# One pool for all eight PSUM banks, and MLP gelus joined to the next mixer gelu, in a planned two-layer attention and mixer kernel

## The chip, the cores and the metric

The kernel runs on one core of a Trainium2 chip. The metric is the device time of one execution in microseconds (us). The kernel before was run three times: 1471.07, 1471.91 and 1472.3 us. Its engines are called PE (matrix products; PEld is its weight load), ACT (ScalarE, table functions), DVE (VectorE), POOL (GpSimd) and SP, which only issues DMAs here.

## What is computed

Two layers, each an attention block and a mixer block, on an input of 2048 rows by 512. The attention has 32 query heads of width 16 and one shared key and value head. The mixer shifts quarters of its features by 1, -1, 2 and -2 rows and ends in an MLP of width 1792. Everything is bf16 at the borders.

```python
def _A_ref(x, wq, wk, wv, wo):                 # S=2048, D=512, H=32, Dh=16
    q = transpose((x @ wq).reshape(B, S, H, Dh), 0, 2, 1, 3)
    k = x @ wk
    v = x @ wv
    scores = einsum("bhqd,bkd->bhqk", q, k) * (Dh ** -0.5)
    p = softmax(scores)
    o = einsum("bhqk,bkd->bhqd", p, v)
    return transpose(o, 0, 2, 1, 3).reshape(B, S, H * Dh) @ wo

def _B_ref(x, w1, w2, w3, w4):
    h = gelu(layernorm(x) @ w1)
    # g0..g3: quarters of h, shifted by 1, -1, 2, -2 rows
    hs = concatenate([g0, g1, g2, g3]) @ w2
    x1 = x + hs
    h2 = gelu(layernorm(x1) @ w3) @ w4
    return x1 + h2

for layer in range(2):
    x = x + _A_ref(layernorm(x), ...)
    x = x + _B_ref(layernorm(x), ...)
```

## The kernel before

**Tiling.** The 2048 rows are 16 tiles of 128. A layer works in chunks of query rows: four of 512 in layer 1, three of 512 and two of 256 in layer 2 (`CHUNKS`, L536). A chunk is eight blocks of four heads (`b`), a block runs over 16 key tiles (`kb`), and each key tile is two halves (`p`) of two heads. A half is therefore 128 keys by 512 queries for two heads: two score matmuls into two PSUM banks of 512 fp32 columns. There are 2048 halves in all.

**Two ways to an exponential.** A half goes one of two ways. As a *unit* (`declare_unit`, L1111) its two score matmuls (L1083, in the profile `PB<-QT,KT`) fill two neighbouring banks and one ACT instruction over 1024 columns writes exp to `EA` (L1127). As a *pair* (`declare_pair`, L1133) each of its two banks is evicted by DVE into a 16-bit integer (`J<-PB`, L1145), which read as bf16 is a rough exponential; two further terms come from integer additions on `J` (`shift_op`, L1182, on POOL, or on DVE while POOL has enough queued), and the three terms are weighted by scaled copies of the values (`VD`). Then the value products (L1232) of both kinds add into one PSUM bank, `ACC`, until the block's last key tile is in.

**The end of a block** (`block_end`, L1240). DVE copies `ACC` to `ACCF` (or adds it to a spilled partial sum: the first chunk of layer 2 starts on early key tiles before layer 1 has ended, L1024 to L1039). Small matmuls (L1285) and a reciprocal turn the sums into factors, DMAs bring the rows into `OT`, and `scale_pair` applies the factors.

**The end of a chunk** (`chunk_end`, L1447). When all eight blocks are in, the rest of the layer for these rows is declared: the output projection, the mixer's first product and gelu (`mixer_in`: W1 products at L676, evicted to `GP` at L1531, one gelu over 4 x 512 columns at L1535), the second product (`mix`), and the MLP (`mlp`: W3 products evicted to `G2` at L1610, a gelu per tile over 1792 columns at L1615, W4 products in `mlp_out`), then, in layer 1, the next layer's keys and values (`next_kv`). A mixer shift needs rows of the next chunk, so the MLP of a chunk covers the tiles that are ripe: three, four, four, then the rest. In the last chunk of layer 2 (`tail`) the gelus read PSUM directly. Exp and gelu need different tables, so a change between them costs a load (`ACT_TABLE_LOAD`).

**Who sets the order.** Nothing of this is a fixed loop. `Plan` is a list scheduler in Python: it keeps modelled clocks of the engines, picks for each engine that is free the ready operation of least priority value, and writes one static instruction stream per engine with semaphore waits. `_pick` (L204) chooses: scores of units have priority 0, scores of pairs 0.5, value products 2, a chunk's projections 10 or less. `limits` and `due` (L291, L306) keep PE from starting work that would make a unit's scores late. `filler` (L1089) adds dummy matmuls (`PB<-ONES,NIL`) when PE's modelled activity falls short. `assign` (L1414) decides when a half becomes a pair, by thresholds that change every 12.5 planned us: the string `TEMPER` (L590) names one of 16 sets of thresholds (`MOODS`) for each stretch.

**Banks.** PSUM has eight banks. Units alternate between banks 0, 1 and 2, 3 (`ACT_SLOTS`); bank 4 is `ACC`, the only accumulator; banks 5, 6 and 7 are a pool for everything else: pair scores, projections, transposes. An operation that takes a bank from the pool (`take`) is placed only when one has been given back (`give`) for a margin of 0.15 us. When all attention work is placed, the units' banks and `ACC` are lent to the pool (`lend`, L317).

Of the kernel before, what the change touches and what calls it, by code (L numbers as in the profile page):

```python
# [27 lines left out]
class Op:  # L28
    __slots__ = ("eng", "emit", "preds", "npend", "succ", "dur", "prio", "seq", "ready", "start",
                 "end", "take", "give", "dma", "out", "pos", "sem", "vc", "side", "placed", "pe", "feeds", "port", "parts", "after", "entry", "weight")  # L30


class Plan:
# [31 lines left out]
    CLOSE = 2.5  # L65
# [4 lines left out]
    BODY = 0.2  # L70

    def __init__(self, nc, pool_banks):
# [29 lines left out]
        self.loose = False  # L102

    def op(self, eng, emit, reads=(), writes=(), dur=0.1, prio=None, take=None, give=None,
# [8 lines left out]
        o.feeds = None  # L113
# [90 lines left out]
    def _pick(self, eng, t, dense=False):  # L204
# [3 lines left out]
        limit = self.limits(t) if eng == "PE" and not dense else ()  # L208
        joins = eng == "PE" and t < self.pe_end - 1e-9
        low = self.deferred(h, t, joins) if eng == "PE" and not dense else {}  # L210
        pressing = joins and any(o.prio == 0 and o.ready <= t + 1e-9 for o in h) and self.pe_kind != "Q"
# [3 lines left out]
        due = list(limit) + self.due(h, t) if stick else ()  # L215
# [4 lines left out]
        for o in h:  # L220
# [13 lines left out]
            key = (low.get(o, o.prio), o.seq)  # L234
            if self.CLOSE and eng == "PE" and o.prio > 2 and o not in low and o.take is None:
                key = (self.CLOSE, o.seq)
# [7 lines left out]
            if o.take is not None:  # L244
                if not all(p.placed and (p.end <= t + 1e-9 or p.eng == "PE") for p in o.take.gates):
                    continue
                margin = self.MARGIN if o.side else self.LAT["PE"]
                k = sorted(i for i in range(len(self.pool)) if self.pool[i][0] + margin <= t + 1e-9)
                k = sorted(sorted(k, key=lambda i: self.pool[i][0])[:o.take.n])
                if len(k) < o.take.n or o.prio > 2 and len(self.pool) <= self.SPARE and self.attach is not None and not self.loose:  # L250
                    continue
# [6 lines left out]
        if o.take is not None:  # L258
            got = [self.pool[i][1] for i in bank]
            for i in reversed(bank):  # L260
                self.pool.pop(i)
            o.take.bank = got[0] if o.take.n == 1 else tuple(sorted(got))
# [28 lines left out]
    def limits(self, t):  # L291

        x = max(t, self.free_at["ACT"])
        res = []
        late = {}
        for u in self.units[-4:]:
            if not u.placed:
                late[u] = x
                x += u.dur
        for o in self.heap["PE"]:  # L300
            if o.prio == 0 and o.ready > t + 1e-9 and o.feeds in late:
                d = late[o.feeds] - o.pe[1] / (2400.0 if self.warm else 1200.0) - 0.17 - self.LAT["ACT"]
                res.append(max(o.ready, d) + self.SLACK)
        return res

    def due(self, h, t):  # L306

        x = max(t, self.free_at["ACT"])
        late = {}
        for u in self.units[-4:]:  # L310
            if not u.placed:
                late[u] = x
                x += u.dur
        return [late[o.feeds] - o.pe[1] / (2400.0 if self.warm else 1200.0) - 0.17 - self.LAT["ACT"]
                for o in h if o.prio == 0 and o.ready <= t + 1e-9 and o.feeds in late]

    def lend(self, banks, o):  # L317

        for b in banks:
            self.pool.append((o.end, b))  # L320
            self.pool_last[b] = o
        heapq.heappush(self.events, o.end + self.MARGIN)
# [187 lines left out]
def t_ps(n):  # L510
    return 0.066 + n * 1.043e-3
# [22 lines left out]
class Kernel:  # L534
# [9 lines left out]
    ACT_SLOTS = (0, 2)  # L544
    ACC = 4
    POOL_BANKS = (5, 6, 7)
# [8 lines left out]
    CALM_END = (2, 1)  # L555
    LATE_OT = 6
# [8 lines left out]
    FREE = 2  # L565
# [24 lines left out]
    TEMPER = "090e357fe7f4ff7e0f7e2eeeff72790e3f75e5ff7145fe87e4c1e43707f90000548fe5eeef9f07ece7eeeff1f0ef9fefee4f897fe741eccccccccc"  # L590
# [1091 lines left out]
```

## Time and profile before

| | us | how to read it |
|---|---|---|
| profiled execution | 1472.13 | one execution, recorded instruction by instruction |
| its span | 1470.2 | first to last instruction; 1.9 lie around it |
| exps, L1127, x1406 | 1292.9 busy | ACT time covered by them; they overlap, one lasts 1.17 on average |
| MLP gelus, L1615, x29 | 47.0 busy | 128 x 1792 each |
| mixer gelus, L1535, x8 | 14.4 busy | seven of 128 x 2048, one of 128 x 1024 |
| table loads, x30 | 38.6 busy | 14 before exps, 8 before mixer gelus, 7 before MLP gelus, one at the start; 1.283 each |
| pair evictions, L1145, x1284 | 821.8 busy | DVE, 0.68 each in the row, overlapping |
| shifts on POOL, L1182, x534 | 976.6 busy | 489 of two rows at 1.90, 45 of one row at 1.06 |
| shifts on DVE, L1182, x136 | 98.6 busy | 125 of two rows at 0.72, 11 of one row at 0.80 |
| fillers, L676 `PB<-ONES,NIL`, x532 | 49.2 busy | dummy matmuls, four at a time |
| first exp starts | 13.99 | |
| last exp ends | 1409.33 | |

Busy time counts an instant once, however many instructions of a group overlap in it, so busy time over count is the step from one to the next where a group runs without gaps, and the mean length of one is longer. The granted clock of PE is 1.00 in every stretch of the run. POOL and DVE do not share work except the shifts.

### The profile page before, as it was taken

Reading aid. Unit: us, or ns where it says so; the run is one execution under the profiler, and the core shown is the slowest. Engines: PE = TensorE matmul, PEld = TensorE weight load, DVE = VectorE, ACT = ScalarE, POOL = GpSimd, SP = SyncE. Lnnn points to the kernel's source line nnn. Section 1 sums busy time; section 2 is a strip of 40 time slices with the busy share of each in tenths; the row PEclk is TensorE's granted clock in tenths of the full one; section 3 lists DMA queues with packets and bytes.
Section 4 is the critical chain, followed back from the end, with each engine's and each line's share of the span. In section 5 each row is a group of like instructions: output and inputs, shape, how many; then the busy total and the mean of one; then the engine's idle time right before and its main releaser. Section 6 shows DMA issues by size and latency. Waiting matters only on the chain.

```text
span 1470.2 us, 65395 instructions
## 1 busy us (share of the span) xinstructions
PE 1446.2 (98%) x29813; PEld 646.8 (44%) x29813; DVE 1295.5 (88%) x2323; ACT 1406.4 (96%) x1496; POOL 1140.3 (78%) x830
## 2 busy tenths in 40 slices
PE   9999999999999999999999999999999999999999
PEld 4344334444443444444444444444433344555565
DVE  8899999989999889998987899999989998889873
ACT  7999999999999999999979999999999999999962
POOL 2888887878898778899854789789769968788951
PEclk9999999999999999999999999999999999999999
DMA  6100100001000000100000000010000000000000
GB/s 217 31 6 6 20 5 7 6 5 20 6 6 5 6 4 6 21 6 2 3 3 3 3 10 10 6 21 5 9 18 8 4 6 8 20 15 7 8 15 24
DMA packets 32662, 21.76 MB, mean 15 GB/s; under 512 B 13056, under 2 KB 31872, under 8 KB 32384
## 3 DMA queue, kind: packets, MB, share of 16 engines
q1 hardware_dynamic: 32384, 17.57, 5.2%
q8 instruction: 233, 3.82, 1.1%
q14 instruction: 45, 0.37, 0.1%
HBM read 7.90 MB, written 2.10 MB: 7 GB/s over the span
## 4 chain that ended last, share of the span: by engine, by line
ACT 73%; PE 22%; DVE 3%; POOL 2%; issue 0%; POOLq 0%
ACT EA L1127 68%; PE PB L676 8%; PE PB L1083 6%; PE PB L1232 6%; ACT G L1615 2%; POOL J L1182 1%; ACT L1127 1%; DVE J L1145 1%; ACT GP L1535 1%; PE PB L876 1%; ACT L1535 1%; ACT L1615 1%; DVE G L1610 0%; PE PB L933 0%; DVE J L1182 0%
## 5 line engine op out<-in xcount | busy, mean ns | idle before, releaser
L1127 ACT ACTIVATE EA<-PB 128x1024 bf16<-128x1024 f32 x1406 | 1292.9, 1172 | 12.3 <-PE PB L1083 6.1
L1182 POOL TENSOR_SCALAR J<-J 128x2048 uint16<-128x2048 uint16 (+1 forms) x534 | 976.6, 1829 | 213.9 <-DVE J L1182 90.1
L1145 DVE TENSOR_SCALAR J<-PB 128x512 uint16<-128x512 f32 x1284 | 821.8, 681 | 81.6 <-PE PB L1083 77.5
L1083 PE MATMUL PB<-QT,KT 32*128 32x512 bf16 (+1 forms) x4608 | 603.0, 360 | 11.7 <-ACT EA L1127 5.0
L1232 PE MATMUL PB<-J,VD 128*32 128x256 bf16 (+1 forms) x8628 | 418.5, 265 | 3.0 <-POOL J L1182 1.1
L1232 PE MATMUL PB<-EA,VP 128*32 128x256 bf16 (+1 forms) x6340 | 343.8, 263 | 1.0 <-DVE QT L1244 0.3
L1083 PEld LDWEIGHTS PB<-QT,KT 32*128 32x128 bf16 x4608 | 162.6, 91 | 383.6 <-ACT EA L1127 313.1
L1232 PEld LDWEIGHTS PB<-J,VD 128*32 128x32 bf16 x8628 | 179.0, 95 | 180.5 <-issue 131.1
L1232 PEld LDWEIGHTS PB<-EA,VP 128*32 128x32 bf16 x6340 | 147.6, 95 | 111.1 <-issue 91.0
L676 PE MATMUL PB<-ZT,W 128*32 128x512 bf16 (+2 forms) x2816 | 168.7, 342 | 0.6 <-DVE ZT L885 0.3
L1182 DVE TENSOR_SCALAR J<-J 128x2048 uint16<-128x2048 uint16 (+1 forms) x136 | 98.6, 725 | 7.2 <-POOL J L1182 6.5
L676 PE MATMUL PB<-W,G 128*32 128x512 bf16 x1624 | 103.5, 380 | 0.0
L1610 DVE CAST G<-PB 128x512 bf16<-128x512 f32 (+2 forms) x126 | 72.2, 581 | 11.4 <-PE PB L676 8.7
L676 PEld LDWEIGHTS PB<-ZT,W 128*32 128x32 bf16 x2816 | 63.8, 96 | 33.4 <-issue 19.3
L812 POOL TENSOR_TENSOR SM<-SM,MH 128x2 f32<-128x2 f32 (+1 forms) x69 | 50.7, 735 | 22.0 <-DVE SM L814 13.3
L1615 ACT ACTIVATE G<-G 128x1792 bf16<-128x1792 bf16 x29 | 47.0, 1686 | 19.5 <-DVE G L1610 19.4
L676 PEld LDWEIGHTS PB<-W,G 128*32 128x32 bf16 x1624 | 38.0, 96 | 37.8 <-issue 11.0
L676 PE MATMUL PB<-ONES,NIL 128*32 128x512 bf16 x532 | 49.2, 407 | 1.4 <-DVE ZT L885 0.4
L792 DVE BATCH_NORM_STATS2 ST<-X 128x6 f32<-128x512 bf16 x64 | 42.9, 678 | 1.6 <-DMA X<-in_A_x_dram 1.3
L1591 POOL TENSOR_TENSOR X<-Y,X 128x512 bf16<-128x512 bf16 x32 | 39.0, 1225 | 6.8 <-DVE Y L1573 5.9
L1268 DVE CAST ACCF<-PB 128x512 bf16<-128x512 f32 (+1 forms) x65 | 40.1, 616 | 3.7 <-PE PB L1232 3.4
L814 POOL TENSOR_SCALAR SM<-MV 128x2 f32<-128x2 f32 (+1 forms) x45 | 12.3, 272 | 31.6 <-DVE MV L794 29.7
(108 smaller groups left out, 767.3 us busy)
## 6 DMA issues: line engine op xcount, KB each, us to landing
OT<-ACCF SPq DMA_DIRECT2D x432, 8.0 KB, 1.8
W<-in_B_w_dram SPq DMA_DIRECT2D x2, 1792.0 KB, 15.0
X<-in_A_x_dram SPq DMA_DIRECT2D x8, 256.0 KB, 5.0
QT<-QS SPq DMA_DIRECT2D x32, 64.0 KB, 2.4
out_dram<-OUTB SPq DMA_DIRECT2D x16, 128.0 KB, 1.7
OT<-ACCF SPq DMA_DIRECT2D x112, 4.0 KB, 2.2
W<-in_B_w_dram SPq DMA_DIRECT2D x2, 512.0 KB, 9.8
WQ<-in_A_wq_dram SPq DMA_DIRECT2D x1, 512.0 KB, 4.6
```

The costliest lines, as they stand in the source:

```text
L676: ins = e.matmul(self.PB[32 * g:32 * g + 32, bank, 0:n], lhsT=lhsT[:, 32 * g:32 * g + 32], rhs=rhs, start=start, stop=stop, tile_position= ...
L792: op("DVE", lambda e, tb=tb: e.bn_stats(self.ST6[:, tb, :], src(tb)), reads=[tagf(tb)], writes=[("ST", tb)], dur=0.606, prio=prio)
L812: op("POOL", lambda e: e.tensor_tensor(out=out, in0=src, in1=self.MH[:, 0, a:b], op=ALU.pow), reads=tags + [("MH",)], writes=tg(r), dur=0. ...
L1083: ins = e.matmul(self.PB[:, bank, j * n:(j + 1) * n], lhsT=self.KT[32 * h:32 * h + 32, la, (kb + j) * 128:(kb + j + 1) * 128], rhs=self.QT ...
L1127: o = q.feeds = op("ACT", lambda e: e.activation(self.EA[:, ea, :, :], self.PB[:, b0:b0 + 2, :], ACTF.Exp, scale=0.25), writes=bk + [("EA" ...
L1145: o = op("DVE", lambda e, i=i, L=L: e.tensor_scalar(out=self.J[:, 3 * s, i * 512:(i + 1) * 512], in0=self.PB[:, L.bank, :], scalar1=128 * ...
L1182: o = self.pl.op(eng, lambda e: e.tensor_scalar(out=self.J[:, d, :], in0=self.J[:, f, :], scalar1=float(self.STEP), scalar2=1.0, op0=ALU.a ...
L1232: ins = e.matmul(self.PB[32 * x:32 * x + 32, self.ACC, p * hw:p * hw + hw], lhsT=v[:, la, kb + j, :], rhs=ap[:, i, j * w + u * hw:j * w + ...
L1268: self.last_copy = op("DVE", lambda e: e.tensor_copy(acc, self.PB[:, self.ACC, 0:n]), writes=[("AC",)] + am, dur=t_ps(n), prio=0, side=False)
L1591: op("POOL", lambda e, tb=tb: e.tensor_tensor(out=self.X[:, tb, :], in0=self.Y[:, tb % 6, :], in1=self.X[:, tb, :], op=ALU.add), reads=[(" ...
L1610: op("DVE", lambda e, f=f, L=L: e.tensor_copy(self.G2[:, f, 0:n], self.PB[:, L.bank, 0:n]), writes=[L] + [(x, f, i) for x in ("G2", "GE") ...
L1615: op("ACT", lambda e, i=i: e.activation(self.G2[:, :, i * 128:(i + 1) * 128], self.G2[:, :, i * 128:(i + 1) * 128], ACTF.Gelu_apprx_tanh), ...
```

## The change

- `ACT_SLOTS` and `ACC` are gone; `POOL_BANKS` is all eight. A unit takes two neighbouring banks when its scores are placed, a block takes an accumulator bank with its first value product and gives it back with the copy to `ACCF`. `lend` goes away, as does the dummy matmul that opened bank 4.
- `couple` picks two neighbouring banks for a unit, `single` one bank for anything else; `single` refuses a bank if taking it would leave no two neighbours free by the time the next unit's scores are due.
- `coming` replaces `limits` and `due`. It walks the units not yet placed and gives for each the latest start of its scores and whether they are urgent. Scores of a unit are placed when urgent, or earlier if PE is already at scores and more than two banks are free.
- The units' scores and exps carry their banks, so value products of one block no longer share a tag with the next.
- `JOINED` names chunks 0, 1 and 2 of layer 2. Their MLP gelus, W4 products and `next_kv` are kept back until the next chunk's mixer gelu, which then waits for both sets of evictions; the MLP gelus follow it without a table load between.
- Several constants of the planner change (`CLOSE`, `FREE`, the assumed length of the L1285 products, four new ones), and `TEMPER` is another string.

```diff
-    CLOSE = 2.5
+    CLOSE = 1.9
...
+    LEAD = 0.4
+    JOIN = 0.7
+    LEFT = 1
+    HORIZON = 1.0
...
-        limit = self.limits(t) if eng == "PE" and not dense else ()
+        coming = self.coming(t) if eng == "PE" and h else ()
+        limit = [max(d, at) + self.SLACK for q, d, at, urgent in coming[:1] if at < 1e8] if not dense else ()
...
+            if o.feeds is not None:
+                urgent = next((x[3] for x in coming if x[0] is o), None)
+                if urgent is None:
+                    continue
+                if not urgent:
+                    if not (self.pe_kind == "Q" and t < self.pe_end + 0.05) or nfree - 2 < self.LEFT:
+                        continue
+                    key = (self.JOIN, o.seq)
...
-                k = sorted(i for i in range(len(self.pool)) if self.pool[i][0] + margin <= t + 1e-9)
-                k = sorted(sorted(k, key=lambda i: self.pool[i][0])[:o.take.n])
-                if len(k) < o.take.n or o.prio > 2 and len(self.pool) <= self.SPARE and self.attach is not None and not self.loose:
+                k = self.couple(t, margin) if o.take.n > 1 else \
+                    self.single(t, margin, None if o.feeds is not None or o.prio in (2, -20) else by)
+                if k is None:
                     continue
...
+    def single(self, t, margin, by):
+
+        f = self.free_banks()
+        best = None
+        for b in range(8):
+            if f[b] + margin <= t + 1e-9:
+                if by is not None:
+                    g = f[:b] + [1e9] + f[b + 1:]
+                    if min(max(g[i], g[i + 1]) for i in range(7)) + self.LAT["PE"] > by + 1e-9:
+                        continue
+                key = (b < 4, f[b], b)
+                if best is None or key < best:
+                    best = key
+        return None if best is None else (best[2],)
+
+    def couple(self, t, margin):
+
+        f = self.free_banks()
+        best = min(((b not in (0, 2), max(f[b], f[b + 1]), b) for b in range(7)
+                    if max(f[b], f[b + 1]) + margin <= t + 1e-9), default=None)
+        return None if best is None else (best[2], best[2] + 1)
+
+    def coming(self, t):
...
+            d = begin - q.pe[1] / rate - 0.17 - self.LAT["ACT"]
+            urge = d - (self.SWITCH if self.pe_kind != "Q" else 0.0) - self.LEAD
+            at, b = min((max(f[i], f[i + 1]), i) for i in range(7))
...
+            res.append((q, d, at, urge <= t + 1e-9))
...
-    ACT_SLOTS = (0, 2)
-    ACC = 4
-    POOL_BANKS = (5, 6, 7)
+    POOL_BANKS = range(8)
...
+    JOINED = ((1, 0), (1, 1), (1, 2))
...
-    FREE = 2
+    FREE = 1
...
-        b0 = self.ACT_SLOTS[k % 2]
+        L = Late(2)
...
-        q = op("PE", fpe, reads=self.inputs(g), writes=bk, pe=("Q", 512, 256, hs), prio=0, side=False)
+        q = op("PE", fpe, reads=self.inputs(g), writes=[L], pe=("Q", 512, 256, hs), prio=0, side=False, take=L)
...
-        op("PE", fpe, reads=rd + ([] if first else [("AC",)]), writes=[("AC",)] if first else [],
-           pe=("P", 256, 256, range(4)), prio=2, side=False)
+        o = op("PE", fpe, reads=rd + ([] if first else [ac]), writes=[ac] if first else [],
+               pe=("P", 256, 256, range(4)), prio=2, side=False, take=A if first else None)
...
-        op("PE", fz, reads=am + [("SELC",)], writes=[L], pe=("P", 100 * nq, 4 * nq, range(4)), prio=fin, take=L)
+        op("PE", fz, reads=am + [("SELC",)], writes=[L], pe=("P", 60 * nq, 4 * nq, range(4)), prio=fin, take=L)
...
         if not tail:
+            kept, self.kept = self.kept, None
             op("ACT", lambda e: e.activation(self.GP[:, par, :, 2:2 + n], self.GP[:, par, :, 2:2 + n],
                                              ACTF.Gelu_apprx_tanh),
-               reads=gt, writes=gt, dur=2.94 + 4 * n / 1200, prio=-1, after=1.4)
+               reads=gt + ([("G2", f, x) for f in range(14) for x in range(4)] if kept else []), writes=gt,
+               dur=(1.54 if kept else 2.94) + 4 * n / 1200, prio=-1, after=0.0 if kept else 1.4)
+            if kept:
+                self.gelus(kept[2], [("GX", f) for f in range(4)])
+                self.mlp_out(kept[0], kept[2])
+                self.next_kv(kept[0], kept[1])
...
+        if not tail:
+            c = self.chunk_of(la, tiles[-1])
+            if (la, c) in self.JOINED:
+                self.kept = la, c, tiles
+                return
+            self.gelus(tiles)
         self.mlp_out(la, tiles, tail)
```

## The prediction

> **What bounds the kernel now.** I read the busy shares first, then the chain that ended last, then ScalarE's waits, then its timeline.
>
> From the page of the kernel before (busy us, share, instructions) and its chain:
>
> ```profile
> PE 1446.2 (98%) x29813; PEld 646.8 (44%) x29813; DVE 1295.5 (88%) x2323; ACT 1406.4 (96%) x1496; POOL 1140.3 (78%) x830
> ...
> ACT 73%; PE 22%; DVE 3%; POOL 2%; issue 0%; POOLq 0%
> ```
>
> PE and ACT both look full. The waits (us in total, times, longest) tell them apart:
>
> ```profile
> PEld PB L1083 <- ACT EA L1127: 313.1, 1082, 0.8
> ...
> ACT G L1615 <- DVE G L1610: 19.4, 3, 12.5
> ...
> PEld PB L1083 <- DVE J L1145: 10.1, 38, 0.5
> ...
> ACT EA L1127 <- PE PB L1083: 6.1, 8, 2.3
> ...
> ACT EA L1127 <- PE PB L1232: 5.8, 3, 5.1
> ```
>
> PE stands 313 us before score matmuls until ACT gives their banks back; ACT waits about 12 us for PE in all. So ACT sets the pace from its first exp (13.99 us) to its last (ends at 1409.33); then a tail of 60.9 us follows in which PE is busy 58.1. ACT's timeline gives the prices (start, us, what, count, idle before):
>
> ```profile
> 741.64 14.77 ACT L1127 ACTIVATE EA<-PB 128x1024 bf16<-128x1024 f32 x16
> 761.55 6.52 ACT L1127 ACTIVATE EA<-PB 128x1024 bf16<-128x1024 f32 x7 [5.14 <-PE PB L1232]
> 768.09 1.28 ACT L1615 ACT_TABLE_LOAD   x1
> 772.99 4.87 ACT L1615 ACTIVATE G<-G 128x1792 bf16<-128x1792 bf16 x3 [3.62 <-DVE G L1610]
> ...
> 1144.74 1.28 ACT L1535 ACT_TABLE_LOAD   x1
> 1146.03 1.91 ACT L1535 ACTIVATE GP<-GP 128x2048 bf16<-128x2048 bf16 x1
> 1147.96 1.28 ACT L1127 ACT_TABLE_LOAD   x1
> 1149.25 104.02 ACT L1127 ACTIVATE EA<-PB 128x1024 bf16<-128x1024 f32 x113
> 1253.29 1.28 ACT L1615 ACT_TABLE_LOAD   x1
> 1254.59 6.46 ACT L1615 ACTIVATE G<-G 128x1792 bf16<-128x1792 bf16 x4
> 1261.06 1.28 ACT L1127 ACT_TABLE_LOAD   x1
> ```
>
> The exps overlap: one lasts 1.18 us (median of the line), but 113 take 104.02, so one more costs (104.02 - 1.18)/112 = **0.918**. A group's last exp costs 0.26 us beyond that step, because the table load waits for its end. A mixer gelu stops the exps from 1144.74 to 1149.25, 4.5 us; an MLP gelu of four tiles from 1253.29 to 1262.36, 9.1; one of three tiles 7.5 (320.53 to 328.00). Between 14 and 1409 us ACT idles some 15 us: 4.05 in the first 36 us (three waits for the first keys), 5.14 and 3.62 at the layer change above, and six waits of 0.2 to 0.6 (2.1 together).
>
> **The change part by part.** The two programs' instruction orders can be set side by side without a time; counts below are from there, durations from the trace.
>
> *Joined gelus.* Three chunks are named, but the order before already runs the last MLP gelu of four tiles directly after the 1.06 us mixer gelu at the end, under one load. Only two joins are new: table loads fall from 30 to 26. A join of four tiles costs 1.30 (load and its gap) + 1.81 (mixer gelu, less the 0.1 by which gelus in a row overlap: three take 4.87, four 6.46, so 1.59 a step against 1.69 for one) + 6.46 + 1.29 = 10.86 in place of 4.51 + 9.07 = 13.58, and one drained exp group less, 0.26: 2.98 saved. Three tiles give the same. Two joins: **-6.0 us**, all on the bound engine. Here a page of the Trainium skill sets another price: "ScalarE: Activation LUTs", section "What ACT_TABLE_LOAD costs", counts the load (about 1.28 us) and a drain of about 1.38, 2.66 per switch; four would be -10.6. The row agrees on the load, 1283 ns, but shows exps starting 1.29 us after the load starts, and only 0.1 to 0.26 of overlap lost before it. I take the trace; the rule would put the time 4.6 us lower.
>
> *Exps.* 1406 become 1401; the five units go as pairs to DVE (1284 evictions at L1145 become 1294): 5 x 0.918 = **-4.6 us**. All five fall before the layer change (763 exps before its three-tile gelu become 758). DVE pays for it: ten evictions at 821.8/1284 = 0.64, 23 more double shifts at 0.72 (POOL does 22 fewer at 1.90), six fewer single ones at 0.80: 6.4 + 16.5 - 4.8 = +18 us. From 36 to 737 us DVE is busy 637 of 701 (91%); with the share of this that falls there (five evictions, 16 double shifts, two single ones fewer: +13) it is 650 of 696, 93%. That is cover, but thin: the second rival.
>
> *The layer change.* Before, scores pause twice: 5.65 us of other matmuls after score matmul 2214 (ACT then idles 5.14), and 8.4 us after 2224, in which the three-tile gelu sits and waits 3.62 for its evictions. In the new order the first pause is gone and the second holds 208 W3 matmuls in a row. The trace prices 16 of these at 0.82 us and 24 at 1.15, so 0.041 each: 8.6 us, and 0.7 until the last eviction is done, 9.3. ACT covers the first 3.1 of it (two exps, one load): about 6.1 us idle in place of 8.76, **-2.7 us**. Bounds: -5 if the evictions land early, +2 if the pause finds only one exp in hand and DVE trails.
>
> *Score banks.* Exps no longer alternate between two fixed pairs of banks. What waits is a score matmul at the head of PE's queue; behind it stand the value products, projections and the next pair's scores, and DVE and ACT wait for those. Before, every exp's scores wait for an exp (1401 such waits). After: 1331 on ACT alone, 32 on ACT and DVE together, and 38 find their banks given back by DVE or long free. So nearly all exps still follow an exp. The trace has no row for the mixed wait. The nearest is PE's wait for DVE at pair scores, 10.1 us in 38 times, 0.27 each, none of which shows as an ACT wait beyond the six short ones. Lower end: those short waits go too, -2. Upper end: all 32 come through at 0.29 (313.1/1082), +9. I take 0, near the row.
>
> *The accumulator bank* joins the pool, so a new block's first value product can open in another bank while DVE still copies the old one: PE stood 4.7 + 1.2 us for that copy, hidden under ACT. Nothing.
>
> *Fillers.* 532 dummy matmuls of 512 columns become 280; at 0.054 each (56 real ones take 3.19, 24 take 1.47) PE loses 13.6 us of empty work. A rule speaks against that: "TensorE: Matmul & The Clock Gate", section "HAM oscillation", says that the clock halves after an idle gap of over about 3.4 us. The trace grants 1.00 in every stretch, PE's longest wait at scores is 0.8 us, and one filler group is four matmuls, 0.2 us; the 88 in the first 14 us stay. By the row this costs 0; by the rule each halved window would add up to 3.4 us of PE time, and four or five windows on ACT's path would eat the gain.
>
> *Start and tail.* The opening order is the same but for one dummy matmul. After the last score matmul PE's work sums to the same: 64 matmuls of 256 columns (1.7 us) are now done earlier, 32 of 512 (1.7) later, 12 more fillers (0.6) wait beside output copies. 0, with 1.5 either way.
>
> Sum: -6.0 - 4.6 - 2.7 = **-13.3 us**. The profiled execution took 1472.13 (span 1470.2 and 1.9 around it), the median of the three runs is 1471.91, which is no different. 1472.1 - 13.3 = 1458.8: I forecast **1459 us**.
>
> **The rivals.**
>
> *The pool does nothing for the exps* (it does not do what it says): 1331 of 1401 still wait for ACT alone, the layer change keeps its 8.8 us idle, and the five exps saved are lost again to short waits. Then only the joins count: 1472.1 - 6.0 = **1466**. For it: DVE rises to 93% in layer 1. Against: the pause after score matmul 2214 is gone from the order.
>
> *DVE becomes what frees the banks, slower than before.* Place: layer 1, 36 to 737 us. A late eviction keeps a bank, a score matmul at PE's head waits for it, and an exp's scores stand behind. 1083 score matmuls carry a wait on DVE, 1120 before. At 0.27 each, 49 waits that come through to ACT eat the 13.3 us, and 60 (one in 18) make the kernel slower by over 0.2%; one in 15 (72) would cost 19.5: 1458.8 + 19.5 = **1478**. For it: DVE has 46 us left in 696. Against: of the 1120 only 38 waited, and ACT's waits for scores were 6.1 us, most of it in the first 36.
>
> *ACT's idle time goes altogether*: with more scores ahead, the 6 us left at the layer change and the 2 us of short waits vanish: 1458.8 - 8 = **1451**. Against: the 208 matmuls in a row stand in the order.
>
> **How the numbers follow.** Forecast 0.60; joins alone 0.20; idle gone 0.07; DVE 0.10; something between, near no change, 0.03. The low end is 1452 (the idle case, nearly); the high end takes the upper end of the score banks, 1459 + 9 = 1468, which holds joins alone. About 0.85 lies within; what is left out is the slow case and the far ends. A measurement here tells changes of over 0.2% (2.9 us) from none: faster 0.86, same 0.04, slower 0.10.
>
> **What would show it.** Table loads 26 and two joined stages of 9.3 and 10.9 us: the joins. Exp groups at 0.918 a step: if they stretch, the score banks cost, and ACT's waits name PE at the score line. One idle gap of about 6 us before the three-tile gelu at the layer change, none of 5 just ahead of it. A tail of 61 us after the last exp. A granted clock under 1.00, or PE's waits for DVE well over 15 us together with new ACT waits in layer 1, would make the forecast wrong.

## The result, and the profile after

| | before | after |
|---|---|---|
| median, us | 1471.77 (1471.07 to 1472.36, 10 runs) | 1467.22 (1461.86 to 1469.79, 10 runs) |
| ratio, 95% interval | | 0.9967 [0.9958, 0.9975] |
| profiled execution, its span | 1472.13, 1470.2 | 1468.02, 1466.2 |
| granted clock, mean of a run | 1.000 in the profiled run and in all 35 repeats beside the experiments | 1.000 in one run, 0.993 to 0.995 in nine |

The changed kernel is faster, by 4.6 us, not by the 13.3 of the forecast. Its runs spread over 8 us where those of before spread over 1.3, and the time goes with the granted clock: 1461.86 at 1.000, 1464.88 to 1468.02 at 0.995 or 0.994, 1468.78 and 1469.79 at 0.993.

From the page of the changed kernel: busy times, the row of the granted clock over 40 slices, and the chain that ended last.

```profile
PE 1436.7 (98%) x29592; PEld 637.1 (43%) x29592; DVE 1306.2 (89%) x2350; ACT 1398.3 (95%) x1487; POOL 1119.0 (76%) x822
...
PEclk9999999999899999999999999999999999999999
...
ACT 62%; PE 30%; DVE 5%; POOL 2%; issue 1%; DMA 0%; POOLq 0%
```

ACT has 8.1 us less work, as it should, but the chain moves from ACT to PE (22% to 30%), and one slice of the clock row is an 8. Before had no such digit:

```profile
PEclk9999999999999999999999999999999999999999
```

The waits of the changed kernel (us in total, times, longest) name the line:

```profile
PEld PB L1127 <- ACT EA L1170: 289.8, 981, 0.6
...
PEld PB L1127 <- DVE J L1190: 13.2, 44, 0.5
...
ACT EA L1170 <- PE PB L1127: 12.5, 21, 1.7
```

L1127 are the scores, L1170 the exps, L1190 the pair evictions. PE still waits for ACT 981 times, so exps still follow exps. But ACT now waits for scores 21 times, 12.5 us, against 8 times and 6.1 before. ACT's timeline shows where seven of these lie:

```profile
379.49 12.47 ACT L1170 ACTIVATE EA<-PB 128x1024 bf16<-128x1024 f32 x13
392.60 1.02 ACT L1170 ACTIVATE EA<-PB 128x1024 bf16<-128x1024 f32 x1 [0.64 <-PE PB L1127]
394.11 1.02 ACT L1170 ACTIVATE EA<-PB 128x1024 bf16<-128x1024 f32 x1 [0.49 <-PE PB L1127]
...
401.57 1.02 ACT L1170 ACTIVATE EA<-PB 128x1024 bf16<-128x1024 f32 x1 [0.70 <-PE PB L1127]
403.31 12.18 ACT L1170 ACTIVATE EA<-PB 128x1024 bf16<-128x1024 f32 x13 [0.71 <-PE PB L1127]
```

From 380 to 391.95 us exps run without a gap, then each waits 0.3 to 0.7 us for its scores, 4.1 us in all. A table of windows over this stretch gives busy us and instructions of PE, PEld, DVE, ACT and POOL, then the granted clock, the DMA share and GB/s:

```profile
384.00:387.40 3.40, 3.40 (x63) 1.53 (x61) 3.40 (x7) 3.40 (x5) 3.00 (x6) 1.00 0.06 12
387.40:390.20 2.80, 2.38 (x35) 0.84 (x34) 2.44 (x6) 2.73 (x4) 2.64 (x3) 1.00 0.00 0
390.20:393.60 3.40, 3.40 (x34) 0.90 (x32) 2.73 (x5) 2.76 (x3) 3.14 (x4) 0.50 0.01 2
...
400.40:403.80 3.40, 3.40 (x62) 1.47 (x52) 1.39 (x3) 1.99 (x3) 2.99 (x2) 0.50 0.02 5
403.80:407.20 3.40, 3.40 (x72) 1.34 (x64) 3.18 (x6) 3.35 (x5) 2.71 (x2) 0.99 0.00 0
```

The clock is half from 390.22 to 403.87, 13.65 us, and there is one more halved stretch of 3.41 us at 219.55. PE is busy all through the halved stretch, and the window ahead of it has 0.42 us without a matmul. So PE had not gone idle for long: it was at work, with 35 matmuls in the 2.80 us ahead of the halving against 63 in the 3.40 before them.

The joins and the layer change, again from ACT's timeline (start, us, what, count, idle before):

```profile
764.61 1.28 ACT L1681 ACT_TABLE_LOAD   x1
772.50 4.87 ACT L1681 ACTIVATE G<-G 128x1792 bf16<-128x1792 bf16 x3 [6.60 <-DVE G L1666]
...
1117.65 1.28 ACT L1586 ACT_TABLE_LOAD   x1
1118.94 1.91 ACT L1586 ACTIVATE GP<-GP 128x2048 bf16<-128x2048 bf16 x1
1120.76 4.85 ACT L1681 ACTIVATE G<-G 128x1792 bf16<-128x1792 bf16 x3
1125.63 1.28 ACT L1170 ACT_TABLE_LOAD   x1
1126.92 1.94 ACT L1170 ACTIVATE EA<-PB 128x1024 bf16<-128x1024 f32 x2
```

One load now serves the mixer gelu and three MLP gelus: exps stop for 1126.92 - 1117.65 = 9.27 us. The join of four tiles takes 10.86 (1293.24 to 1304.10). At the layer change one idle gap of 6.60 us is left.

### The profile page after: what moved, and what is told of

It is laid out like the page before. It is cut to its first block, busy times and chain, and to the rows that moved or that the text cites. A ratio compares the mean times of both kernels' runs of the same rounds, so it can differ in the third digit from the quotient of the medians.

```text
span 1466.2 us, 64989 instructions
## 1 busy us (share of the span) xinstructions
PE 1436.7 (98%) x29592; PEld 637.1 (43%) x29592; DVE 1306.2 (89%) x2350; ACT 1398.3 (95%) x1487; POOL 1119.0 (76%) x822
## 4 chain that ended last, share of the span: by engine, by line
ACT 62%; PE 30%; DVE 5%; POOL 2%; issue 1%; DMA 0%; POOLq 0%
ACT EA L1170 59%; PE PB L1127 9%; PE PB L720 9%; PE PB L1281 9%; DVE J L1190 2%; ACT G L1681 2%; POOL J L1227 1%; PE PB L918 1%; ACT L1170 1%; DVE ST L834 1%; PE PB L1051 1%; ACT GP L1586 1%; DVE J L1227 0%; PE PB L975 0%; DVE G L1666 0%
## 5 line engine op out<-in xcount | busy, mean ns | idle before, releaser
L1170 ACT ACTIVATE EA<-PB 128x1024 bf16<-128x1024 f32 x1401 | 1290.2, 1162 | 13.1 <-PE PB L1127 12.5
L1227 POOL TENSOR_SCALAR J<-J 128x2048 uint16<-128x2048 uint16 (+1 forms) x526 | 953.8, 1813 | 241.9 <-DVE J L1227 113.9
L1190 DVE TENSOR_SCALAR J<-PB 128x512 uint16<-128x512 f32 x1294 | 830.1, 681 | 70.1 <-PE PB L1127 65.2
L1127 PE MATMUL PB<-QT,KT 32*128 32x512 bf16 (+1 forms) x4608 | 604.8, 361 | 11.1 <-ACT EA L1170 4.1
L1281 PE MATMUL PB<-J,VD 128*32 128x256 bf16 (+1 forms) x8676 | 414.2, 265 | 7.5 <-POOL J L1227 4.1
L1281 PE MATMUL PB<-EA,VP 128*32 128x256 bf16 (+1 forms) x6324 | 355.9, 266 | 1.5 <-DVE J L1190 0.6
L1127 PEld LDWEIGHTS PB<-QT,KT 32*128 32x128 bf16 x4608 | 162.4, 91 | 384.7 <-ACT EA L1170 289.8
L1281 PEld LDWEIGHTS PB<-J,VD 128*32 128x32 bf16 x8676 | 187.6, 95 | 143.0 <-issue 94.6
L1227 DVE TENSOR_SCALAR J<-J 128x2048 uint16<-128x2048 uint16 (+1 forms) x153 | 109.5, 717 | 7.1 <-POOL J L1227 6.6
L720 PE MATMUL PB<-WO,OT 128*32 128x512 bf16 x512 | 37.8, 381 | 0.9 <-issue 0.9
L1707 DVE TENSOR_TENSOR OUTB<-PB,X 128x512 bf16<-128x512 f32 x16 | 11.0, 688 | 27.7 <-PE PB L720 27.7
```

What stands on the lines that cost most here:

```text
L720: ins = e.matmul(self.PB[32 * g:32 * g + 32, bank, 0:n], lhsT=lhsT[:, 32 * g:32 * g + 32], rhs=rhs, start=start, stop=stop, tile_position= ...
L1127: ins = e.matmul(self.PB[:, bank, j * n:(j + 1) * n], lhsT=self.KT[32 * h:32 * h + 32, la, (kb + j) * 128:(kb + j + 1) * 128], rhs=self.QT ...
L1170: o = q.feeds = op("ACT", lambda e: e.activation(self.EA[:, ea, :, :], self.PB[:, L.bank[0]:L.bank[0] + 2, :], ACTF.Exp, scale=0.25), writ ...
L1190: o = op("DVE", lambda e, i=i, L=L: e.tensor_scalar(out=self.J[:, 3 * s, i * 512:(i + 1) * 512], in0=self.PB[:, L.bank, :], scalar1=128 * ...
L1227: o = self.pl.op(eng, lambda e: e.tensor_scalar(out=self.J[:, d, :], in0=self.J[:, f, :], scalar1=float(self.STEP), scalar2=1.0, op0=ALU.a ...
L1281: ins = e.matmul(self.PB[32 * x:32 * x + 32, A.bank, p * hw:p * hw + hw], lhsT=v[:, la, kb + j, :], rhs=ap[:, i, j * w + u * hw:j * w + u ...
```

## The experiments

The working theory was that the clock is what took the gain, and that it halves where little of the array works. To have a number for "little", I counted from the matmul records the share of the array at work in each window of 3.413 us (the halved stretches in the traces are one to six times that long). Scores load 32 of 128 rows, the tiled products 32 of 128 columns, so each covers a quarter of the array; 512 columns over all of it are counted as 0.213 us. The trace agrees: 88 tiled matmuls last 0.43 us longer than 80, two fills of the array. A filler group of four, 0.213 us, is then worth 0.0625 of a window. By this count the lowest window of before, at any starting point between 36 and 1400 us, has 0.36. In the changed kernel there are windows of 0.31 to 0.34 near 216, 385 and 1165 us.

The planner of both kernels holds the same rule as an assumption, which the prediction did not use. Its constants are `WINDOW = 3.4133`, `WARM = 0.40` and `STAY = 0.36`; `roll` plans PE at half speed after a window in which less than the share `STAY` was at work, counted as here, and `idle` asks for a filler when the planned share falls short of `KEEP`, 0.55. The plan keeps modelled clocks, though, and the chip its own: the changed order falls under 0.36 in the trace.

**More filler everywhere.** Ahead of value products in 14 sparse ranges (counted in score matmuls), every fourth call adds a filler group, 93 in all. The order of the rest is the same.

```diff
+            if not first and any(x <= self.nq < y for x, y in self.LOW):
+                self.nadd += 1
+                if self.nadd % self.EACH == 0:
+                    self.dot(e, A.bank, 512, self.NIL, self.ONES, False, False)
```

> The changed kernel with 93 more filler groups (four dummy matmuls of 512 columns each), put ahead of value products only in the stretches where its trace shows the lowest share of the array at work; the order of everything else is the same. Theory A (the halved clock in two stretches, 219.6 to 223.0 and 390.2 to 403.9 us, takes most of the missing gain, and it comes because the array's share of work falls, not because PE idles): granted clock 1.000 in every run, times within 1 us of each other, median 1461 to 1463. Rival B (the waits in that stretch come from banks that DVE frees late, the clock only goes along): 1467 or more, since PE gets 20 us more to do. Rival C (the clock halves at random): clock below 1.000 in most runs as before.

Measured: 1469.12 (1468.52 to 1470.54, 11 runs), ratio 0.9986 [0.9977, 0.9994]. The clock was 1.000 in ten runs and 0.999 in the profiled one, and the gaps between 390 and 404 us shrink to 0.18. The spread falls to 2 us. But 93 groups are 20 us of PE work in stretches where PE has little to spare. The clock came out as theory A had it and the time as rival B had it, so this run alone does not decide between them; the low dose below, with the same lines and 16 groups, does. The clock can be held; the dose was too large.

**The changed kernel with thin fillers.** Its 70 filler groups keep their places but stream 4 columns in place of 512.

```diff
-            "PE", lambda e: self.dot(e, (L or A).bank, 512, self.NIL, self.ONES,
+            "PE", lambda e: self.dot(e, (L or A).bank, 4, self.NIL, self.ONES[:, 0:4],
```

> The changed kernel with its 70 filler groups cut from 512 to 4 columns, order unchanged. Theory A: the fillers that were left held the clock in part of the places; without them more windows of 3.4 us run at half clock, granted clock below 0.99, time above 1470. Rival B or C: PE has 15 us less empty work, 1467 or a little less, clock 0.994 as before.

Measured: 1465.22 (1460.85 to 1468.45, 4 runs), ratio 0.9955 [0.9938, 0.9973]. Run by run: 1460.85 at clock 1.000, 1462.40 at 0.998, 1468.03 and 1468.45 at 0.993. That is not the fall to under 0.99 that theory A expected: the few fillers that the changed kernel has left do little for its clock. The profiled run is the one at 1.000, so it shows the changed order without a halved stretch between the exps; I use it below for the sum. Its opening is another matter. The same 16 matmuls take 1.05 us in the changed kernel and 1.90 here:

```profile
10.37 1.05 PE L1051 MATMUL PB<-YT,WQ 128*32 128x512 bf16 x16
```

```profile
10.49 1.90 PE L1051 MATMUL PB<-YT,WQ 128*32 128x512 bf16 x16 [0.52 <-DVE YT L927]
```

The clock row reads 1.00 there all the same, because the record of the clock begins only at 15.51 us in this profile (at 4.51 in the changed kernel's, at 7.55 in that of before).

**The kernel before with thin fillers**, the same edit there, 532 of them.

> The kernel before with its 532 dummy matmuls kept in place but cut from 512 columns to 4, nothing else moved. Without the fillers' columns the trace of before has stretches of 3.4 us in which only 0.20 to 0.28 of the array is at work (lowest 0.203; with them the lowest is 0.36), and 1.6% of such stretches lie under 0.34, against 0.5% in the changed kernel. Theory (fillers hold the clock where scores crowd): the granted clock falls below 1.00 in nearly every run, to 0.98 to 0.995, and the time rises by 2 to 10 us, to 1474 to 1481. Rival (the clock follows something of the changed order, not the fillers): clock 1.000 in all runs, 1471.5 or up to 1 us less.

Measured: 1491.9 (1490.2 to 1494.73, 4 runs), ratio 1.0138 [1.0124, 1.0152], clock 0.976 to 0.978 in every run. This is the run that decides: nothing but the columns of the dummies differs from before. The page's row of the granted clock:

```profile
PEclk9997999999999999999999979999997999999999
```

ACT's timeline of this kernel at the first 7 of that row:

```profile
109.61 18.61 ACT L1127 ACTIVATE EA<-PB 128x1024 bf16<-128x1024 f32 x20
128.42 1.02 ACT L1127 ACTIVATE EA<-PB 128x1024 bf16<-128x1024 f32 x1 [0.19 <-PE PB L1083]
129.64 2.12 ACT L1127 ACTIVATE EA<-PB 128x1024 bf16<-128x1024 f32 x2 [0.20 <-PE PB L1083]
132.67 1.02 ACT L1127 ACTIVATE EA<-PB 128x1024 bf16<-128x1024 f32 x1 [0.92 <-PE PB L1083]
134.18 1.02 ACT L1127 ACTIVATE EA<-PB 128x1024 bf16<-128x1024 f32 x1 [0.49 <-PE PB L1083]
```

It is the picture of the changed kernel at 392 us. Dummy work that I had priced at nothing holds the clock of the kernel before, and without it 71.7 us are spent at half clock in the profiled run, and the median is 20.2 us longer. The direction was expected, the size was underrated two to ten times.

**A low dose.** The same four lines as in the first experiment, in three ranges only (around 216 to 223, 385 to 404 and 1165 us): 16 groups.

```diff
+    LOW = ((645, 668), (1148, 1196), (3388, 3400))
+    EACH = 4
```

> The changed kernel plus a filler group of four matmuls ahead of every fourth value product, in three stretches only: those where the trace of the changed kernel was halved or has its lowest array share (around 216 to 223, 385 to 404 and 1165 us). Theory (low array share there is what halves the clock): clock 1.000 in most runs, 1461 to 1464, spread under 3 us. Rival (halving strikes wherever the share is under some 0.37, so other stretches take its place): clock 0.995 to 0.999 in most runs, 1464 to 1468. Rival (the halving has nothing to do with the share): 1467 to 1469 with clock 0.993 to 0.995.

Measured: 1463.28 (1462.07 to 1464.56, 5 runs), ratio 0.9942 [0.9928, 0.9955], clock 1.000 in all runs. The profile of this kernel holds no record of the clock, but its timeline agrees: between 390 and 404 us exps wait twice, 0.18 and 0.17 us, where they waited seven times and 4.1 us in the changed kernel.

**A quarter of the dose.** Of each added group only one matmul.

```diff
-                    self.dot(e, A.bank, 512, self.NIL, self.ONES, False, False)
+                    e.matmul(self.PB[0:32, A.bank, :], lhsT=self.NIL[:, 0:32], rhs=self.ONES, start=False, stop=False,
+                             tile_position=(0, 0), skip_group_check=True)
```

> The kernel with 16 added filler groups in the three sparse stretches (1463.3, clock 1.000), but of each added group only one of its four matmuls: 128 rows by 32 columns instead of 128 by 128, the same 512 columns of stream. Theory (the clock goes by the share of the array at work): a quarter of the added share is not enough, the clock falls to 0.993 to 0.997 in most runs and the time is 1465 to 1469. Rival (any matmul other than scores, or PE's time on them, does it): clock 1.000, 1462 to 1463.5, as less work is added.

Measured: 1462.31 (1461.85 to 1462.58, 5 runs), ratio 0.9937 [0.9924, 0.9949], clock 1.000 in all runs. This is the fastest kernel of the study, with 16 matmuls added. I had expected the clock to fall; clock and time are those that the rival had named. The count shows why the share allows it too: two or three such matmuls come into one window, 0.016 each, and lift the lowest windows there to 0.36; the lowest of the run is 0.346, near 260 us. So the run fits the share, but it doesn't tell it from any other reckoning of PE's work. Windows of 100 us for before, after and this kernel, in this order (columns as above):

```profile
300.00:400.00 100.00, 99.10 (x1922) 42.79 (x1914) 92.19 (x164) 99.94 (x107) 80.20 (x62) 1.00 0.06 11
```

```profile
300.00:400.00 100.00, 99.03 (x1846) 41.61 (x1846) 89.86 (x163) 97.11 (x103) 77.91 (x61) 0.95 0.06 11
```

```profile
300.00:400.00 100.00, 99.22 (x1925) 43.85 (x1923) 91.93 (x166) 99.51 (x106) 79.94 (x62) 1.00 0.06 11
```

PE's busy share is 99% in all three and tells nothing. ACT tells it: 99.94, 97.11, 99.51 us busy.

**Thin fillers and a low dose.** Old fillers cut to 4 columns after the opening, 20 groups added in five ranges (two more, around 260 and 628 us).

> The changed kernel with its own fillers cut to 4 columns after the opening (first 100 score matmuls) and 20 filler groups added in five sparse stretches (the three of the kernel with added groups, and those around 260 and 628 us, which fall to 0.33 once the old fillers are thin). Theory (only windows under some 0.34 to 0.36 of the array halve the clock, fillers elsewhere are idle cargo): clock 1.000, 1460 to 1462.5, the fastest of all. Rival (fillers elsewhere are cover too): clock under 0.998 in most runs, 1464 or more. If the old fillers cost nothing beside the exps: 1463, as the kernel with added groups.

Measured: 1462.92 (1462.09 to 1464.32, 5 runs), ratio 0.9943 [0.993, 0.9955], clock 1.000 in three runs and 0.999 in two. The old fillers cost nothing beside the exps: with them cut the kernel is not faster than the low dose.

**All profiles together.** Thirteen of the fourteen profiled executions (all but the low dose's) have a record of the clock. They hold 5155 windows of 3.413 us, on the grid on which the clock changes, between 36 and 1400 us, that ran at full clock themselves. They can be sorted by the share of the array at work in the window, each matmul's work counted at its start:

| share in the window | windows | of these followed by half clock |
|---|---|---|
| under 0.33 | 11 | 11 |
| 0.33 to 0.36 | 5 | 1 |
| 0.36 to 0.39 | 19 | 3 |
| over 0.39 | 5120 | 0 |

The share tells nearly every case, and the three of 0.36 to 0.39 (two of them the changed kernel's, at 0.375) are about the uncertainty of the count: with each matmul's work spread over the time that it streams, the first three rows become 10 of 10, 3 of 4 and 2 of 22. PE's busy time does not sort the same windows. Those that led to half clock were busy for 0.49 to 0.88 of their length, and 189 others that were no busier than 0.88 led to nothing. The sum of streamed columns sorts them almost as well as the share, since nearly every matmul here covers a quarter of the array. In the profiles the grid stands differently to the first instruction in each execution, so where a sparse stretch falls in it differs. That is the likely reason why the same changed kernel runs at 1461.9 and at 1469.8; it is not shown, as each kernel has one profile.

**One part alone.** The pool without joins, at the changed thresholds (`JOINED = ()`):

> The changed kernel with no chunk joined (banks, planner constants and thresholds as changed; 1408 exps, 32 table loads). Theory A: layer 1 is planned as in the changed kernel, so its clock halves there too; the joins' 2.8 us each and one more load at the end are lost: 1467 + 7 exps x 0.92 + 6 loads' worth (about 8) = 1480. The prediction's sum (without the clock): 1459 + 6 + 6 = 1471. If the pool alone is a gain, it is under 1472.

Measured: 1483.59 (1478.82 to 1489.45, 6 runs), ratio 1.0087 [1.0069, 1.0105]. 1408 exps, six loads more than the changed kernel, and new stalls in layer 2 (one of 1.97 us, seven of 0.4 to 0.8). Clock 1.000 in two runs, 0.990 to 0.995 in four.

The joins on the old banks and old thresholds (`JOINED`, `gelus` and the kept group moved into the kernel before):

> The kernel before with the three chunks joined and nothing else (two fixed score slots, three pool banks, old thresholds; 1411 exps, 26 table loads). Prediction's step: 1471.8 - 2 x 2.8 + 5 exps x 0.92 = 1470.8 if the planner's order else costs the same; the clock stays 1.000 as before. If the joins cost elsewhere (later W4 products, a tail that waits for both evictions): 1473 or more.

Measured: 1494.7 (1494.03 to 1496.03, 4 runs), ratio 1.0159 [1.0146, 1.0172], clock 0.999 to 1.000. The joined stage itself is as short as forecast, 9.27 us from 1134.32. What follows it is new; ACT's timeline of this kernel:

```profile
1137.43 4.85 ACT L1634 ACTIVATE G<-G 128x1792 bf16<-128x1792 bf16 x3
1142.30 1.28 ACT L1129 ACT_TABLE_LOAD   x1
1143.59 12.94 ACT L1129 ACTIVATE EA<-PB 128x1024 bf16<-128x1024 f32 x14
1161.78 20.27 ACT L1129 ACTIVATE EA<-PB 128x1024 bf16<-128x1024 f32 x22 [5.25 <-PE PB L1234]
1183.32 19.36 ACT L1129 ACTIVATE EA<-PB 128x1024 bf16<-128x1024 f32 x21 [1.27 <-PE PB L1234]
1206.88 3.77 ACT L1129 ACTIVATE EA<-PB 128x1024 bf16<-128x1024 f32 x4 [4.20 <-PE PB L1234]
```

Here exps wait for value products (L1234), 12.3 us in four gaps, three of them shown (the fourth, 1.59, is at 1303.10). The other engines' timelines give the chain at the first: POOL's last three shifts of the old block end at 1159.91, its last value product starts at 1160.01, DVE copies `ACC` from 1160.71 to 1161.38, the next block's first value products start at 1161.43 after a wait of 0.82 for that copy, and the exp, which waits for them, at 1161.78. With the one pool the next block need not wait for the copy: from the start of a block's last value product to the start of the next block's first it is 1.62 us on average in before and 1.55 here, and 0.72 in the changed kernel with thin fillers, where in 54 of 72 ends the next block's products run during the copy. But the copy and the wait for it take about 1.4 of the 5.25 us here; the late shifts come before it, and what made them late is not shown. The tail is 8.9 us longer than before's too.

The changed kernel with the old string `TEMPER`, and the pool alone with it:

> The changed kernel whole, with joins and one pool, but the thresholds of before. Same 1434 exps and 1228 pair evictions as the kernel with the pool and the old thresholds and no joins, 26 loads in place of 32: the pair differs by the three joins alone. Joins at 2.98 each on the bound engine: 6 to 9 us less than that kernel. If joins cost as much as they save by crowding PE and DVE behind the longer gelu stage: within 2 us of it, or above it. Clock 1.000, with 636 fillers. By the exps' pace 33 x 0.918 = 30 us above the changed kernel.

> One pool of all banks, no joins, and the thresholds that decide pairs as in the kernel before: what the pool does by itself. Its order has 1434 exps (before 1406), 32 loads (before 30) and 648 fillers. If exps set the pace here too: 28 x 0.918 + 2 x 1.3 = 28 us more, 1500, clock 1.000. If the pool itself speeds the exps (forecast's exps step as the pool's own): 1467 or less. If the longer plan has idle ACT in it: over 1500, with ACT waits for PE at the score line.

Measured: 1520.63 (1518.82 to 1522.18, 4 runs) and 1523.58 (1519.41 to 1524.68, 4 runs). Both lie over 20 us above the 1500 that the exps' pace would give; ACT idles 29.1 and 36.7 us between first and last exp, against 15.9 in before. Between the two the joins alone are worth 3.0 us, less than the 6 to 9 expected: the last mixer gelu then waits 15.55 us for both sets of evictions (1462.63), and the tail is 15.5 us longer. Part of the 3.0 is not the joins', as the clock differs too (0.994 to 0.998 with them, 0.992 to 0.996 without).

The kernel before with the new string alone:

> The kernel before with nothing changed but the string of thresholds, taken from the changed kernel. Its order has 1426 exps (before 1406), 32 loads (before 30) and 1033 fillers. By the exps' pace 20 x 0.918 + 2 x 1.3 = 21 us more: 1493, clock 1.000. If the thresholds carry the changed kernel's gain by themselves (five exps fewer): 1467 or less. If the string fits only the structure it was chosen for: 1490 to 1525, as the changed kernel does with the old string (1520.6).

Measured: 1547.61 (1546.8 to 1548.33, 4 runs), above all that was expected. The exps explain 18 of the 76 us; ACT's idle time between first and last exp grows from 15.9 to 68.8, with single waits of 10.0, 11.3, 9.0 and 6.6 us.

None of these five kernels, which pair a string with a structure other than its own, comes out even: they are 0.9% to 5.2% slower than before. So no part of the change can be priced by taking it out.

**The third join.** The low dose with chunk 2 not joined.

```diff
-    JOINED = ((1, 0), (1, 1), (1, 2))
+    JOINED = ((1, 0), (1, 1))
```

> The kernel with 16 added filler groups, with chunks 0 and 1 of layer 2 joined, not chunk 2. The order up to the last exp is the same (1401 exps, 344 fillers); table loads 28 in place of 26, both behind the last exp. Forecast's view (before already ran this gelu under the same load, so the third join gives nothing and PE bounds the tail): 1463.3 within 1.5. Rival (the third join makes the last mixer gelu wait 4.2 us for both sets of evictions, and that delays the tail): 1459.5 to 1461.5. Rival (two more loads on the tail's path): 1465 to 1466.

Measured: 1462.6 (1461.92 to 1466.24, 5 runs), against 1463.28 of the low dose (1462.07 to 1464.56): no difference. ACT's timelines, first with three joins, then with two:

```profile
1399.29 1.28 ACT L1594 ACT_TABLE_LOAD   x1
1404.72 1.06 ACT L1594 ACTIVATE GP<-GP 128x1024 bf16<-128x1024 bf16 x1 [4.15 <-DVE G L1674]
1405.68 6.44 ACT L1689 ACTIVATE G<-G 128x1792 bf16<-128x1792 bf16 x4
```

```profile
1401.80 1.28 ACT L1689 ACT_TABLE_LOAD   x1
1405.10 6.46 ACT L1689 ACTIVATE G<-G 128x1792 bf16<-128x1792 bf16 x4 [2.02 <-DVE G L1674]
```

The MLP gelus start within 0.6 us of each other either way, because both wait for the same evictions. The two extra loads do not both lie behind the last exp, as had been expected, but ahead of it: without the third join the last mixer gelu stands among the exps, at 1370.86 between two loads. The last exp ends 2.5 us later (1401.78 against 1399.27) and the tail is 3.0 us shorter (59.1 against 62.1), so the two cancel.

Not tried: the one pool with a single accumulator, and the joins on old banks with the new string.

## Why the prediction was wrong, step by step

ACT's time can be added up in four terms, from the traces of before, of the changed kernel with thin fillers (clock 1.000 behind the opening), of the changed kernel with 16 added matmuls (clock 1.000), and of the changed kernel as profiled:

| us against before | forecast | thin fillers | 16 added matmuls | as profiled |
|---|---|---|---|---|
| start of the first exp | 0 | +1.4 | -0.2 | -0.5 |
| ACT busy, first to last exp | -10.6 | -9.5 | -8.5 | -8.0 |
| ACT idle in it | -2.7 | -3.7 | -1.7 | +3.8 |
| tail after the last exp | 0 | +0.6 | +0.7 | +0.7 |
| sum (span) | -13.3 | -11.2 | -9.7 | -4.0 |

The +1.4 belongs to the thin fillers of the opening and not to the changed order: in the kernel with thin fillers and a low dose, where the opening's fillers are whole, the first exp starts at 13.47 and not at 15.43.

- **The step that failed is the fillers**: "By the row this costs 0". The row was the granted clock of 1.00 in every stretch of before. But that row was measured with the 532 fillers in place, and they were its cause: without them before falls to 0.976 to 0.978 and loses 20.2 us. The changed order keeps 280, and its clock is halved in a few stretches; 16 added matmuls bring it back to 1.000. The text had the alternative, "four or five windows on ACT's path would eat the gain", and five windows it was in the profiled run, 17.07 us at half clock. They cost some 6 us (1468.02 as profiled against 1461.86 in the run at 1.000), 1.2 each, not 3.4. At half clock a window of 3.4 us can withhold no more than 1.7 us of PE's work, so the 3.4 was too high as a sum; that ACT felt less than the 1.7 fits slack that PE had elsewhere. At full clock the changed kernel gains 9.9 us (1461.86); the rest of the 13.3 is in the smaller terms below.
- The prediction weighed the rule of the Trainium skill, "TensorE: Matmul & The Clock Gate", section "HAM oscillation", by its words: an idle gap of over some 3.4 us. No gap ahead of a halving comes near that. A window of that length in which PE works, but with about a third of the array or less, does the same: in the 15 windows that led to a halving PE stood still for 0.40 to 1.74 us in all, and its longest pause was 1.72. The rule was the better guide than the row, though its condition is not what was met; the `STAY` of the planner, in the code of both kernels, names a condition that is nearer to it.
- **Joins**: right. Stages of 9.27 and 10.86 us, as worked out; the loads between first and last exp cover 5.1 us less. The third makes no difference to the time, as the forecast had it, but by two effects that cancel. On the disputed price of a table switch the trace stands: exps start 1.29 us after a load starts. The 0.26 us of a drained group was too high, since a lone exp lasts 1.02 us and not 1.18: 1.02 - 0.918 is 0.10. A join saves 2.8 us, not 2.98.
- **Exps**: right in sign, a little large: -4.1 us of exp time with thin fillers and -3.2 with 16 added matmuls, for the -4.6 forecast.
- **Layer change**: right. Idle 6.60 us for about 6.1, and the gap of 5.14 is gone: -2.2 for the -2.7 forecast.
- **Score banks at nothing**: right at full clock, within about 1 us. With 16 added matmuls PE waits 13.8 us for pair evictions, 44 times, against 10.1 and 38, and ACT waits 7.0 us for scores, 16 times, against 6.1 and 8. The second rival, DVE freeing banks late, did not come.
- **Accumulator bank at nothing**: right for the sum. It may hide a dependence: with joined gelus on the one accumulator, ACT idled 12 us behind value products in the experiment. That kernel also had the old banks and thresholds, so the cause is not shown.
- **Joins alone, 1466**, the rival nearest to the measured time, was not the cause: the exps and the layer change brought their part, and the clock took some 6 us back. That 1467 lies near 1466 is chance.

With the 16 added matmuls the kernel takes 1462.31, 9.1 us less than before. That is the forecast's mechanism with the clock held. Its profile has 3.6 us less than the 13.3: 2.1 in ACT's busy time (1.4 of them the exps), 1.0 in its idle time and 0.7 in the tail, less 0.2 at the start.

## What to carry to other kernels

A row of the profile is measured under conditions that a change may remove: before costing dummy work at nothing, ask whether the row that says so depends on it, take it out of the kernel before to see, and read in the code why it was put there. When PE is sparse, count its matmuls in windows of 3.4 us, weighted by the part of the array that they cover, rather than its busy share, and place filler only where that count is low; two or three quarter-array matmuls to a window were enough here. Here the table of thresholds belonged to one structure: parts of a change that share such a table have no price of their own.

## What was not expected of the hardware

The clock halved while PE was at work for half to nine tenths of the window before, in steps of 3.413 us: after all 11 windows with under 0.33 of the array at work, after 4 of 24 between 0.33 and 0.39, after none of 5120 over 0.39. That lies near the 0.36 of the planner's `STAY`, a number in the code that the kernel before rarely put to the test, as its lowest window has 0.36. One instruction order then takes 1461.9 to 1469.8 us, probably as the sparse stretches fall in the steps. Two or three added matmuls of a quarter of the array, running beside value products, lift a window enough; whether the chip counts cells, columns or something else isn't told by these runs, since scores and tiled products cover a quarter each. And half clock is not half speed for the kernel: in the profiled run of before with thin fillers 71.7 us of it cost 23.0 us (1494.73 against 1471.73), or 0.32 us for each, 1.2 of the 23.0 being the later start of the exps; PE is busy 97% of that span.
